# Fewer TensorE transposes and low-word pieces, per-head exponentials and a new order in a fused attention and SoLU kernel

## The chip, the cores and the metric

The kernel runs on one core of a Trainium2 chip. The metric is device time in microseconds (us). PE is TensorE, DVE VectorE, ACT ScalarE, POOL GpSimd, SP SyncE, whose queue here issues the loads and the DMA transposes. SBUF is the on-chip memory, and PSUM the accumulators that TensorE writes.

## The reference

Chunked attention over 4 batches, 8 heads, 768 positions, head size 64, followed by a SoLU layer. Every chunk of 32 queries sees 8 memory keys and a window of 16 + 32 + 8 keys (64 in all).

```python
for c in range(nc):                                   # 24 chunks of 32 queries
    scores = scale * q_c @ k_full.T                   # k_full: memory + window
    a = np.exp(scores - max(scores))
    out[c] = (a / (sum(a) + 1e-9)) @ v_full
x = out as (3072 tokens, 512)
h = x @ w_in                                          # 512 -> 1024
solu = h * softmax(h)
ln = (solu - mean) / sqrt(var + 1e-6) * g_ln
return ln @ w_out                                     # 1024 -> 512
```

All tensors are float32. The kernel uses a faster matmul type of 32 bits that keeps fewer mantissa bits, so that each operand of the two dense products is split in a high and a low part, and three products are summed.

## The kernel before

The 3072 tokens make 24 tiles of 128. Attention works on 13 units: tiles 0 and 1 alone, then pairs of tiles. The whole program is one list of steps, written out by hand in a string called `ORDER` and executed in that order under a manual schedule: every engine gets its instructions in the order in which the steps name them, and semaphores hold back an instruction whose data or buffer is not ready. The number in a step is its unit, tile or weight piece; the letter after @ is its engine (V DVE, S ACT, G POOL, Y SP).

Weights come in 16 pieces of 128 x 512 elements (0 to 7 of `w_in`, 8 to 15 of `w_out`), each element as 8 bytes, the two 32-bit words of a double. Steps on a piece `i`:

- `D` loads the raw words (512 KB). `A` (ACT, `w_pack`) and `B` (DVE, `w_first`) make the leading value from the high word, `E` (DVE, `w_exp`) its power of two.
- `H` (`w_high`) writes the rounded high part, for `w_out` scaled by `g_ln`.
- `T` (DVE, `w_word`) makes the contribution of the low word in one instruction with two factors.
- `R` (`w_rest`) adds value, minus high part and low word in PSUM by three matmuls of 512 columns with identity or diagonal matrices; `W` (ACT) copies the sum to the low part. There are two such PSUM buffers.
- For the other pieces `K`, `Y` and `J` do the same by element-wise steps on POOL or DVE without PE.

Attention steps of a unit: `S` scores, `M` row maxima, `Bm` scores minus maximum, `X` exponentials in place, `Z` their sums and inverses. Then the probabilities are transposed, either on PE (`PT`, with `PC` copying the result from PSUM) or by a DMA transpose (`Ps` splits the words in two planes of 16 bits, `Px` is the DMA, `Pm` joins the planes). `V` multiplies by the values, `N` normalises, and the result is transposed in the same two ways (`XT`, or `Xs`, `Xx`, `Xm`) and split in high and low parts (`XH`, `XL`).

Dense steps of a tile: `G` is the first product in four parts by `w_in` (12 matmuls of 128 x 512 for two halves, a quarter of the depth each: 6 per part); `Hm`, `He`, `Hu`, `Sq`, `C` are maximum, exponential, product with sums, squares, and centring; `UT`, or `Us`, `Ux`, `Um`, transposes; `UH`, `UL` split; `O` is the second product in eight parts of three matmuls; `Os` and `St` scale and store.

Buffers of one kind are handed out first in, first out in program order: 12 SBUF `slot` tiles, 8 rounded tiles `fr`, 3 PSUM tiles `two`, 2 PSUM tiles `one`, and two each for q, k and v. A step that takes a buffer waits until its previous user has finished.

Of the kernel before, what the change touches and what calls it, by code (L numbers as in the profile page):

```python
# [35 lines left out]
W3@S M2 G1.0 D8 G0.0 W2@S B4 E5 H5@S G1.1 Bm2 A6 E4 T5 H4@S A7 Lk4@Y B6 T4 X2 G0.1 R4 R5 D9 Z2 S3
H6@S D10 B7 E6 A9 E7 T7 W4@S T6 R6 W5@S M3 H7@S G1.2 A8 Lv2@Y B8 Bm3 G0.2 E8 R7 B9 Lq4@Y PT2 D11
W6@S X3 E9 W7@S T8 A10 T9 PC2 H9@S Z3 G0.3 Hm0 H8@S D12 V2 B10 A11 G1.3 Lq5@Y D13 N2 E10 He0 A12 XT2
Hm1 A13 B11 R8 K10@G H10@S R9 Hu0 Y10@G E11 XH2@S Sq0 B12 He1 XL2@V PT3 K11@V Dn0@G PC3 Lk6@Y S4
Lv3@Y E12 C0 Hu1 B13 G2.0 M4 G2.1 Lv4@Y K12@G H11@S T10 H12@S Sq1 Y12@G E13 K13@G G2.2 Bm4 V3 G2.3  # L40
Lk5@Y J10@G T12 C1 X4 H13@S W8@S N3 G3.0 W9@S XT3 G3.1 G3.2 Hm2 Ps4.0@S Z4 Lv5@Y Y11@G XH3@S XL3@V
Y13@G J12@G Ps4.1@G D14 Dn1@G Lq7@Y G3.3 He2 Hu2 Px4 UT0 D15 T11 Sq2 Hm3 UH0@S J11@G He3 C2 UL0@V
G4.0 Dn2@G Pm4.0@G G4.1 Us2.0@S A14 T13 O0.0 A15 Hu3 Us2.1@G S5 O0.1 Sq3 Pm4.1@S B14 G4.2 E14 B15
Ux2 O0.2 J13@G Dn3@G E15 G4.3 K14@V H14@S UT1 O0.3 K15@G T14 M5 O0.4 Bm5 H15@S UH1@S Y14@G Y15@G
O0.5 J14@V UL1@V Um2.0@G V4 N4 Um2.1@G X5 Ps5.0@S UH2@G Ps5.1@S Xs4.0@S Xs4.1@S T15 O0.6 G5.0 O1.0
J15@V G5.1 Lq6@Y O1.1 Hm4 C3 Us3.0@S G5.2 Px5 He4 Z5 O1.2 Xx4 O1.3 Us3.1@G O0.7 G5.3 Pm5.0@G UL2@V
Os0 Hu4 Sq4 O1.4 Hm5 Ux3 S6 Lk7@Y O2.0 Xm4.0@G O1.5 O2.1 Lk8@Y C4 He5 Lv6@Y Pm5.1@G O1.6 St0 Xm4.1@S
Dn4@G O2.2 O2.3 O2.4 M6 Us4.0@G O1.7 Um3.0@S Bm6 XH4@G O2.5 V5 X6 Um3.1@G Os1 Ps6.0@S Us4.1@G UH3@S
Ux4 XL4@V Hu5 N5 O2.6 Sq5 UL3@V G6.0 O2.7 Z6 G6.1 S7 G7.0 C5 Ps6.1@G Xs5.0@S Px6 Xs5.1@S Dn5@G G6.2
Xx5 O3.0 G6.3 Us5.0@S Us5.1@G Os2 Um4.0@S G7.1 O3.1 St1 Pm6.0@S Hm6 Um4.1@G He6 G7.2 UH4@S Xm5.0@S  # L50
Pm6.1@G O3.2 Hu6 G7.3 Xm5.1@G Sq6 O3.3 UL4@V O3.4 Ux5 Um5.0@G V6 Hm7 O4.0 C6 Lq8@Y O3.5 XH5@S O3.6
Um5.1@S XL5@V Dn6@G O4.1 N6 Us6.0@S He7 Hu7 St2 UH5@S O3.7 UL5@V Xs6.0@G G8.0 Sq7 Us6.1@G O4.2 G8.1
# [622 lines left out]
```

## Time and profile before

| | |
|---|---|
| median of 3 runs | 352.19 us (351.4 to 353.33) |
| profiled execution | 352.38 us, span 350.6 us, mean clock 0.983 |
| PE | 338.9 us busy (97%), 4368 matmuls |
| DVE, ACT, POOL | 230.2, 203.4, 201.5 us busy |
| DMA | 62.90 MB, mean 179 GB/s |
| first product of the dense layer starts | 27.14 us |
| PE is idle between 27 us and the last matmul | 2.1 us in all |

The profiled execution lies 0.2 us above the median, and its time 1.8 us above its span, the part before the first and after the last instruction. A matmul on PE overlaps its neighbours, so the distance from one start to the next is read as its cost, and the listed duration is longer.

### The profile page before, as it was taken

The page shows a single profiled execution, that of the slowest core. Times are in us where ns is not written, and L with a number is a line of the kernel's source. Part 1 is how long each engine was busy: PE and PEld are TensorE (multiplying, and loading weights), DVE is VectorE, ACT ScalarE, POOL GpSimd, SP SyncE. Part 2 cuts the span into 40 slices and gives each one's busy share as a digit, 9 for nine tenths or more (in the row PEclk, how much of TensorE's full clock was granted, in tenths as well). Part 3 has the DMA queues.
Part 4 walks back from the last instruction along what each step waited for, and adds up shares of the span by engine and source line. Part 5 has one row for each costly group of instructions (what it writes and reads, how often), then busy time and mean ns, then how long its engine had stood idle before and what let it go on. Part 6 is the DMA issues. An engine that isn't in the chain of part 4 may idle for free.

```text
span 350.6 us, 9994 instructions
## 1 busy us (share of the span) xinstructions
PE 338.9 (97%) x4368; PEld 269.4 (77%) x4368; DVE 230.2 (66%) x298; ACT 203.4 (58%) x265; POOL 201.5 (57%) x231
## 2 busy tenths in 40 slices
PE   7599999999999999999999999999999999999995
...
PEclk9679999999999999999999999999999999999999
...
GB/s 230 409 310 407 284 345 118 283 125 113 201 254 190 143 84 194 339 158 166 218 209 197 263 192 153 227 130 169 245 89 68 60 91 107 76 127 53 2 90 60
DMA packets 96907, 62.90 MB, mean 179 GB/s; under 512 B 82528, under 2 KB 82528, under 8 KB 96864
## 3 DMA queue, kind: packets, MB, share of 16 engines
...
## 4 chain that ended last, share of the span: by engine, by line
PE 88%; DVE 7%; DMA 2%; ACT 1%; issue 1%; SPq 0%
PE one L570 39%; PE two L509 35%; PE two L400 9%; PE one L309 2%; DMA slot<-in_w_in 2%; PE two L380 2%; DVE per_row L518 1%; DVE slot L533 1%; DVE slot L470 1%; DVE slot L551 1%; DVE fr L301 1%; DVE fr L229 1%; PE one L310 1%; PE one L311 1%; SPq L236 0%
## 5 line engine op out<-in xcount | busy, mean ns | idle before, releaser
L223 POOL TENSOR_SCALAR slot<-slot 128x1024 uint16<-128x1024 uint16 x94 | 119.5, 1297 | 53.6 <-DVE slot L551 16.2
L570 PE MATMUL one<-w_out_h,fr 128*128 128x512 f32 x384 | 133.8, 399 | 0.0
L509 PE MATMUL two<-w_in_h,fr 128*128 128x512 f32 x384 | 133.4, 398 | 0.3 <-ACT two L541 0.3
L509 PEld LDWEIGHTS two<-w_in_h,fr 128*128 128x128 f32 x384 | 72.2, 188 | 17.8 <-ACT two L541 0.5
L570 PEld LDWEIGHTS one<-w_out_h,fr 128*128 128x128 f32 x384 | 72.2, 188 | 17.6
L221 ACT COPY slot<-slot 128x1024 uint16<-128x1024 uint16 x62 | 71.7, 1195 | 15.7 <-DVE slot L551 10.0
L509 PE MATMUL two<-w_in_l,fr 128*128 128x512 f32 x192 | 75.7, 394 | 0.0
L570 PE MATMUL one<-w_out_l,fr 128*128 128x512 f32 x192 | 75.7, 394 | 0.0
L518 DVE TENSOR_REDUCE per_row<-two 128x1 f32<-128x1024 f32 x24 | 29.3, 1222 | 41.0 <-PE two L509 41.0
L229 DVE TENSOR_TENSOR fr<-slot,fr 128x1024 fp32r<-128x1024 f32 x30 | 45.6, 1526 | 6.0 <-PE one L570 2.1
L523 ACT ACTIVATE slot<-two,per_row 128x1024 f32<-128x1024 f32 x24 | 26.8, 1116 | 38.8 <-DVE per_row L518 36.5
L509 PEld LDWEIGHTS two<-w_in_l,fr 128*128 128x128 f32 x192 | 36.2, 188 | 8.1
L570 PEld LDWEIGHTS one<-w_out_l,fr 128*128 128x128 f32 x192 | 36.1, 188 | 8.0
L578 ACT ACTIVATE o_sb<-one,per_row 128x512 f32<-128x512 f32 x24 | 16.4, 685 | 34.5 <-PE one L570 34.5
L541 ACT ACTIVATE two<-slot,per_row 128x1024 f32<-128x1024 f32 x24 | 26.8, 1118 | 13.9 <-DVE per_row L536 13.8
L533 DVE CUSTOM_DVE_ANT_0 slot<-two,slot 128x1024 f32<-128x1024 f32 x24 | 29.2, 1215 | 8.1 <-ACT slot L523 8.0
L551 DVE TENSOR_SCALAR slot<-slot,per_row 128x1024 f32<-128x1024 f32 x24 | 23.2, 965 | 11.1 <-ACT two L541 11.1
L470 DVE TENSOR_TENSOR slot<-two,per_head 128x1024 f32<-128x1024 f32 (+1 forms) x13 | 14.8, 1140 | 11.3 <-PE two L400 11.3
L400 PEld LDWEIGHTS two<-v,slot 64*32 64x32 f32 x1536 | 16.6, 108 | 5.6 <-issue 4.8
L319 POOL TENSOR_SCALAR slot<-slot,g_col 128x512 f32<-128x512 f32 x4 | 3.3, 821 | 29.7 <-DVE slot L284 28.1
L400 PE MATMUL two<-v,slot 64*32 64x64 f32 x1536 | 19.0, 232 | 0.7 <-issue 0.7
L400 PEld LDWEIGHTS two<-k,q 64*32 64x32 f32 x1536 | 16.4, 105 | 4.3 <-issue 3.3
...
## 6 DMA issues: line engine op xcount, KB each, us to landing
...
k<-in_kw SPq DMA_DIRECT2D x11, 672.0 KB, 5.2
out<-o_sb ACTq DMA_DIRECT2D x24, 256.0 KB, 2.4
q<-in_qT SPq DMA_DIRECT2D x11, 512.0 KB, 4.8
slot<-in_w_in SPq DMA_DIRECT2D x8, 512.0 KB, 9.1
slot<-in_w_out SPq DMA_DIRECT2D x8, 512.0 KB, 5.6
v<-in_vw SPq DMA_DIRECT2D x2, 512.0 KB, 10.8
k<-in_kw SPq DMA_DIRECT2D x2, 336.0 KB, 4.6
```

Source lines behind the costliest of these rows:

```text
L221: nc.scalar.copy(out, in_)
L223: nc.gpsimd.tensor_scalar(out, in_, 1.0, 0.0, ALU.mult, ALU.add)
L229: either(on).tensor_tensor(out, a, b, ALU.subtract)
L400: nc.tensor.matmul(out[32 * j:32 * j + 32, r, t, g], *pairs(slice(r * D, (r + 1) * D), t, g, j), start=True, stop=True,)
L470: nc.vector.tensor_tensor(x, heads(u, get("xp", u), D).rearrange("p r t g n -> p r (t g) n"), rinv.broadcast_to([P, 2, n, D]), ALU.mult,)
L509: nc.tensor.matmul(h[:, half], x[a], w[b][:, c, half * HALF:(half + 1) * HALF], start=c == 0 and i == 0, stop=c == NC_ - 1 and i == 2,)
L518: nc.vector.tensor_reduce(take("per_row", ("hm", t), 1), flat(get("h", t)), axis=AX.X, op=ALU.max, negate=True)
L523: nc.scalar.activation(take("slot", ("u", t), 3), flat(get("h", t)), AF.Exp, bias=get("hm", t), scale=1.0, accum_out=take("per_row", ("esu ...
L533: nc.vector.tensor_tensor_reduce(u, flat(get("h", t)), u, 1.0, 0.0, ALU.mult, ALU.add, accum_out=usum)
L541: nc.scalar.activation(flat(get("h", t)), get("u", t), AF.Square, bias=get("nmu", t), scale=1.0, accum_out=take("per_row", ("var", t), 1),)
L551: nc.vector.tensor_scalar(u, u, get("nmu", t), None, ALU.add)
L570: nc.tensor.matmul(get("o", t), u[a], w[b][:, f], start=f == 0 and i == 0, stop=f == NF - 1 and i == 2)
```

## The change

- `PT2`, `PT3` (probabilities of units 2 and 3) and `UT0`, `UT1` (tiles 0 and 1 of the dense layer) become DMA transposes: `Ps`, `Px`, `Pm` and `Us`, `Ux`, `Um`. `UT23`, `PT0`, `PT1` and the four `XT` stay.
- Pieces 8 and 9 lose `R` and `W` and go the way of `K`, `Y`, `J`; the diagonal matrices `Dg` go.
- Units 0 and 1 use `Mh` (maxima, times the scale), `Xh` (an exponential instruction for each of 8 heads, 64 wide, straight from PSUM with a bias and a sum) and `Zh` (inverses) for `M`, `Bm`, `X`, `Z`.
- The low word of five pieces (3 to 7) goes to POOL in two instructions, `Tc` (word to float, scaled, in place) and `Tp` (times the power of two). Nine of the `H` go from ACT to POOL (before none).
- `C` may run on POOL (4 of 24 do), with two operations in the instruction for one. 14 `slot` tiles for 12.
- `ORDER` is another list throughout.

```diff
-SLOTS, ROUNDED = 12, 8
+SLOTS, ROUNDED = 14, 8
-SCALED = range(10, 16)
+SCALED = range(8, 16)
 ORDER = """
-CT Lq0@Y Lq1@Y Lk0@Y Lk1@Y Wu16 D0 D1 A0 Lv0@Y S0 D3 Lv1@Y D2 S1 M0 Lg Bm0 D4 M1 X0 A1 Bm1 Z0 Lq2@Y
+Lk0@Y CT Lk1@Y Lq0@Y Wu16 S0 Mh0 D3 A3 Xh0 B3 Lq1@Y D7 PT0 A7 PC0 D1 E3 S1 Lv0@Y V0 A1 B7 E7 Zh0 Mh1
...
+    def w_word_f32(i, on):
+        f = piece(i)[3]
+        factor = g_word[:, f:f + 1] if i in SCALED else 2.0**-52
+        low = word(i, 0)
+        if on == "S":
+            nc.scalar.activation(low.bitcast(F32), low, AF.Copy, scale=factor)
+        else:
+            either(on).tensor_scalar(low.bitcast(F32), low, factor, 1.0, ALU.mult, ALU.mult)
+
+    def w_word_exp(i, on):
+        p = get("a", i)[:, HALF:]
+        t = take("fr", ("t", i), 1)[:, 0:HALF]
+        either(on).tensor_tensor(t, word(i, 0).bitcast(F32), p, ALU.mult)
+        used("raw", i)
...
+    def exps_by_head(u):
+        s = heads(u, get("s", u), KEYS)
+        nmax = per_head(u, get("nmax", u))
+        sums = per_head(u, take("per_head", ("rinv", u), 1))
+        n = len(UNITS[u]) * NP_
+        a = take("slot", ("p", u), 2)[:, 0:2 * n * KEYS]
+        for i in range(n):
+            for r in range(2):
+                k = 2 * i + r
+                nc.scalar.activation(
+                    a[:, k * KEYS:(k + 1) * KEYS], s[:, r, i // NP_, i % NP_], AF.Exp,
+                    bias=nmax[:, r * n + i:r * n + i + 1], scale=scale, accum_out=sums[:, k:k + 1],
+                )
...
+    def scaled_max(u):
+        row_max(u)
+        nmax = per_head(u, get("nmax", u))
+        nc.vector.tensor_scalar(nmax, nmax, scale, None, ALU.mult)
+
+    def inverses(u):
+        s = per_head(u, get("rinv", u))
+        nc.vector.tensor_scalar(s, s, 1e-9, None, ALU.add)
+        nc.vector.reciprocal(s, s)
...
-    def u_center(t):
+    def u_center(t, on):
         u = get("u", t)
-        nc.vector.tensor_scalar(u, u, get("nmu", t), None, ALU.add)
+        if on == "S":
+            nc.scalar.activation(u, u, AF.Identity, bias=get("nmu", t), scale=1.0)
+        else:
+            either(on).tensor_scalar(u, u, get("nmu", t), 0.0, ALU.add, ALU.add)
```

The order on PE, from the warm-up on, before. `two` and `one` are the PSUM tiles, k, q, v the inputs; L400 are scores (from k, q) and values (from v), L380 transposes, L309 to L311 the three matmuls of an `R`, the end of the list is `S2`.

```order
L400 MATMUL two_81<-k_88,q_86 32x64 x32
L400 MATMUL two_82<-k_89,q_87 32x64 x32
L380 MATMUL two_83<-ident,slot_66 128x128 x4
L380 MATMUL two_81<-ident,slot_69 128x128 x4
L400 MATMUL two_82<-v_90,slot_70 32x64 x32
L380 MATMUL two_83<-ident,slot_70 128x128 x4
L400 MATMUL two_81<-v_91,slot_66 32x64 x32
L309 MATMUL one_84<-slot_63,ident 128x512
...
L400 MATMUL two_81<-k_88,q_86 32x64 x64
```

The same place now (L418 for L400, L398 for L380, L327 for L309):

```order
L418 MATMUL two_83<-k_90,q_88 32x64 x32
L398 MATMUL two_84<-ident,slot_63 128x128 x4
L418 MATMUL two_85<-k_91,q_89 32x64 x32
L418 MATMUL two_83<-v_92,slot_66 32x64 x32
L327 MATMUL one_86<-slot_62,ident 128x512
L328 MATMUL one_86<-w_in_h,eye_neg 128x512
L329 MATMUL one_86<-fr_76,eye 128x512
L418 MATMUL two_84<-k_90,q_88 32x64 x64
L398 MATMUL two_83<-ident,slot_71 128x128 x4
L327 MATMUL one_87<-slot_65,ident 128x512
```

The scores of unit 1 now come after the transpose of unit 0, and the scores of unit 2 after one `R` for three; in all seven `R`, for four, and also `S3`, stand ahead of the first `G`.

On POOL, after the constants, before (the first rows make `g_word` and the diagonal matrices, then comes `K10`):

```order
L200 TENSOR_SCALAR g_word<-g_col 128x8
L204 TENSOR_SCALAR diag<-ident,g_col 128x128
L205 TENSOR_SCALAR diag_r<-ident,g_col 128x128
...
L319 TENSOR_SCALAR slot_62<-slot_62,g_col 128x512
L324 TENSOR_TENSOR slot_62<-slot_62,w_out_h 128x512
```

And now (L314 is `Tc`, L319 `Tp`, L225 to `w_in_h` is `H`):

```order
L314 TENSOR_SCALAR slot_61<-slot_61 128x512
L225 TENSOR_SCALAR w_in_h<-slot_62 128x512
L319 TENSOR_TENSOR fr_76<-slot_61,slot_62 128x512
...
L319 TENSOR_TENSOR fr_82<-slot_63,slot_67 128x512
L225 TENSOR_SCALAR w_in_h<-slot_74 128x512
L319 TENSOR_TENSOR fr_77<-slot_66,slot_64 128x512
L225 TENSOR_SCALAR slot_70<-slot_71 128x1024
L202 TENSOR_SCALAR g_word<-g_col 128x8
```

Sixteen instructions on weight pieces of `w_in`, and one of the two planes for `Px2`, now stand ahead of what was first on POOL.

On SP, the issues of loads and transposes from the 24th on, before:

```order
L236 DMA v_90<-in_vw 128x2x1024
L236 DMA q_86<-in_qT 128x2x512
L268 DMA slot_61<-in_w_out 128x1024
L268 DMA slot_66<-in_w_out 128x1024
L236 DMA q_87<-in_qT 128x2x512
```

And now:

```order
L270 DMA slot_62<-in_w_out 128x1024
L238 DMA q_88<-in_qT 128x2x512
L270 DMA slot_71<-in_w_out 128x1024
L379 DMA_TRANSPOSE slot_61<-slot_70 128x16x128
L238 DMA v_92<-in_vw 128x2x1024
L270 DMA slot_64<-in_w_out 128x1024
L379 DMA_TRANSPOSE slot_73<-slot_74 128x16x128
```

Two transposes (`Px2`, `Px3`) stand among the loads of `w_out` and v; before, the first transpose was the 37th issue.

More of the change, by code (lines that the diff above doesn't have):

```diff
@@ L36 @@
[L36 to L52, printed above, removed]
@@ L88 @@
-Os19 O21.0 O21.1 O20.5 UH23@S Dn23@G UL23@V O21.2 O20.6 O21.3 O20.7 Os20 O21.4 O21.5 O22.0 O21.6
-O22.1 Dn22@G O21.7 O22.2 O22.3 St20 Os21 O23.0 O22.4 O23.1 O22.5 O23.2 St21 O23.3 O23.4 O22.6 O23.5
-St19 O22.7 Os22 O23.6 St22 O23.7 Os23 St23
+Lk0@Y CT Lk1@Y Lq0@Y Wu16 S0 Mh0 D3 A3 Xh0 B3 Lq1@Y D7 PT0 A7 PC0 D1 E3 S1 Lv0@Y V0 A1 B7 E7 Zh0 Mh1
+D0 B1 Tc3@G E1 T1 H3@G A0 B0 N0 Tp3@G H7@G Lq2@Y Xh1 Tc7@G D2 A2 Lk2@Y Zh1 B2 E0 Tp7@G R3 S2 E2 D4
+XT0 D6 A4 R7 W3@S H1@S D5 A6 A5 T0 H0@G Lq3@Y W7@S T2 R0 Lk3@Y M2 XH0@S Bm2 B5 PT1 B6 B4 Tc6@G W0@S
@@ new lines @@
+Tc4@G R1 S3 Lv1@Y E5 Lg PC1 Tc5@G H5@G H4@G X2 Tp5@G D10 D9 Ps2.0@S E4 D11 E6 H6@S Tp4@G H2@G V1 R5
+W1@S XL0@V R4 W5@S Lk4@Y Z2 A10 N1 Tp6@G Ps2.1@G M3 B10 A9 XT1 XH1@S Bm3 D15 B9 A11 X3 W4@S R2 Dw
+E10 Lq4@Y B11 E9 E11 G0.0 R6 K9@G H9@G K11@G A15 W2@S D13 W6@S S4 XL1@V G0.1 G0.2 G0.3 T10 T9 B15
+Px2 Lv2@Y Ps3.0@S T11 M4 E15 Ps3.1@S Z3 D8 A13 Px3 Pm2.0@S Bm4 K10@G Y9@G Pm2.1@S G1.0 H10@S K15@G
+J9@G A8 X4 H11@G Lv3@Y Hm0 He0 V2 Lv4@Y T15 G1.1 B13 N2 Y10@G XT2 XH2@S Z4 D12 Hu0 XL2@V Sq0 Pm3.0@G
@@ new lines @@
+Y11@G Pm3.1@G G1.2 G1.3 V3 Hm1 Ps4.0@G B8 He1 A12 Lk6@Y E13 C0@G N3 Lq5@Y Hu1 G2.0 G2.1 J10@G E8
+Ps4.1@S XT3 Lk5@Y Px4 Sq1 K13@G G2.2 XH3@S Us0.0@G Us0.1@S T13 C1@G Us1.0@S G2.3 K8@G S5 B12 T8 E12
+Pm4.0@S XL3@V Hm2 J11@G G3.0 G3.1 M5 He2 Bm5 G3.2 G3.3 Us1.1@G Ux0 H15@G Pm4.1@S Lk7@Y Ux1 Y15@G
+H8@S V4 Hu2 Lq6@Y Sq2 G4.0 K12@V H13@S G4.1 Um0.0@G Hm3 N4 G5.0 He3 Um0.1@G T12 Y13@G Xs4.0@G X5
+UH0@S Y8@V Lv7@Y H12@S Hu3 Xs4.1@S J8@V Um1.0@G Um1.1@G Ps5.0@S Dn1@G D14 UL0@V Y12@V G5.1 Sq3
+Ps5.1@S Lq7@Y C2@V Us2.0@G UH1@S G4.2 O0.0 G4.3 O0.1 J12@V Xx4 A14 C3@G Us2.1@G G5.2 J13@V S6 Hm4
```

89 lines of the change are left out of this document (50 added, 39 removed).

## The prediction

> **What bounds the kernel now.** I read first the page's shares, slices and clock, then the chain that ended last, then PE's waits.
>
> ```profile
> PE 338.9 (97%) x4368; PEld 269.4 (77%) x4368; DVE 230.2 (66%) x298; ACT 203.4 (58%) x265; POOL 201.5 (57%) x231
> PE   7599999999999999999999999999999999999995
> PEclk9679999999999999999999999999999999999999
> PE 88%; DVE 7%; DMA 2%; ACT 1%; issue 1%; SPq 0%
> ```
>
> PE is full from the third slice on and the chain runs through it. From about 18 us the end moves with the amount of work in PE's list and with PE's few waits; what DVE, ACT and POOL do counts only where PE waits for them. Those waits, from 45 to 110 us (later slices are full):
>
> ```profile
> PE two L400 <- issue: 0.7, 1, 0.7
> PE two L380 <- ACT two L541: 0.7, 1, 0.7
> PE two L380 <- DVE slot L470: 0.4, 1, 0.4
> PE two L509 <- ACT two L541: 0.3, 1, 0.3
> ```
>
> 2.1 us is all that better ordering behind the head can win. What is left is work taken off PE, and the head, where PE waits for loads.
>
> **Work taken off PE.** From the chain (start, length), `PT2` and `UT1`; from the timeline, the stretch with `R8`, `R9`, `PT3` and then `S4`, and `UT0` and the `G` behind it:
>
> ```profile
> 42.71 0.87 PE two L380 x8
> ...
> 79.92 0.87 PE two L380 x8
> ```
>
> ```profile
> 48.72 1.02 PE L309 MATMUL one<-slot,diag 128*128 128x512 f32 x2
> 52.26 1.09 PE L380 MATMUL two<-ident,slot 128*128 128x128 f32 x8 [0.72 <-ACT two L541]
> 53.28 1.48 PE L400 MATMUL two<-k,q 64*32 64x64 f32 x128
> 69.04 1.03 PE L380 MATMUL two<-ident,slot 128*128 128x128 f32 x8
> 70.34 0.50 PE L509 MATMUL two<-w_in_h,fr 128*128 128x512 f32 x1 [0.27 <-ACT two L541]
> ```
>
> `PT2` and `UT1` are 0.87 each. From 48.72 to 53.28 all is removed: 4.56, of it two `R` at about 1.3 each, a transpose, and 0.72 of waiting for the transpose's PSUM buffer. `UT0` takes 70.34 - 0.27 - 69.04 = 1.03. Together 0.87 + 0.87 + 4.56 + 1.03 = 7.3 us. The 0.27 in front of `G4.0` is a wait for a buffer that the dense layer itself holds; I keep it.
>
> **The head.** In-order loads set it. Sizes, and when loads of the kernel before had landed (ACT waiting for the third and fifth weight piece, then issue and landing of the k of units 2 and 3):
>
> ```profile
> k<-in_kw SPq DMA_DIRECT2D x11, 672.0 KB, 5.2
> ...
> q<-in_qT SPq DMA_DIRECT2D x11, 512.0 KB, 4.8
> slot<-in_w_in SPq DMA_DIRECT2D x8, 512.0 KB, 9.1
> ...
> v<-in_vw SPq DMA_DIRECT2D x2, 512.0 KB, 10.8
> k<-in_kw SPq DMA_DIRECT2D x2, 336.0 KB, 4.6
> ...
> q<-in_qT SPq DMA_DIRECT2D x2, 256.0 KB, 2.8
> ```
>
> ```profile
> 14.89 0.66 ACT L274 ACTIVATE slot<-slot 128x512 f32<-128x512 f32 x1 [1.41 <-DMA slot<-in_w_in]
> ...
> 18.88 0.68 ACT L274 ACTIVATE slot<-slot 128x512 f32<-128x512 f32 x1 [0.20 <-DMA slot<-in_w_in]
> ```
>
> ```profile
> L236 SPq DMA_DIRECT2D k<-in_kw x1: 379/379/379, 13.6 to 13.6; - x1
> ...
> DMA to landing us min/median/max: 9.4/9.4/9.4
> ```
>
> ```profile
> L236 SPq DMA_DIRECT2D k<-in_kw x1: 433/433/433, 21.7 to 21.7; - x1
> ...
> DMA to landing us min/median/max: 7.5/7.5/7.5
> ```
>
> Added up in issue order, these are 3232 KB at 14.9, 4768 at 18.9, 6464 at 13.6 + 9.4 = 23.0 and 8672 at 21.7 + 7.5 = 29.2: a straight line of some 390 KB per us. In the new list v of unit 0 ends at 3232 KB (14.9), k of unit 2 at 5440 KB (20.5), k of unit 3 at 8160 KB (27 to 28) and v of unit 1 at 8672 KB (28.3 to 29.2; the old line lost about 1 us to an issue that waited for an SBUF slot, and there are two more slots now).
>
> PE's own rows of the head: the first `R` at a low clock (twice the 1.02 of 48.72), scores of unit 2, the first `G`.
>
> ```profile
> 18.21 2.07 PE L309 MATMUL one<-slot,ident 128*128 128x512 f32 x2
> ...
> 24.30 1.48 PE L400 MATMUL two<-k,q 64*32 64x64 f32 x128
> ...
> 27.14 0.39 PE L509 MATMUL two<-w_in_h,fr 128*128 128x512 f32 x1
> ```
>
> The per-head exponentials, priced from full-width rows: plain 512 and 1024 wide, with bias 1024 wide, and the read of the sum.
>
> ```profile
> L440 ACT ACTIVATE slot<-slot 128x1024 f32<-128x1024 f32 x11 | 11.7, 1059 | 11.1 <-DVE slot L431 11.1
> ...
> L440 ACT ACTIVATE slot<-slot 128x512 f32<-128x512 f32 x2 | 1.2, 622 | 0.0
> ```
>
> ```profile
> L523 ACT ACTIVATE slot<-two,per_row 128x1024 f32<-128x1024 f32 x24 | 26.8, 1116 | 38.8 <-DVE per_row L518 36.5
> ...
> L523 ACT ACTIVATION_READ_ACCUMULATOR slot<-two,per_row 128x1 f32 x24 | 4.6, 192 | 0.0
> ```
>
> 437 ns for 512 columns leave about 185 ns fixed; with 57 for the bias and 55 for 64 columns one is 0.30 us, plus 0.19 for the read, at most 8 x 0.49 = 3.9 us a unit; neighbours on ACT overlap by about 0.1, twice here, so at least 8 x 0.26 = 2.1. I take 2.3, since it is many short ones in a row. The old path of a unit (`Bm`, `X`) is one instruction on DVE and 0.62 on ACT, so `PT0` comes 1 to 2 us later. It does not matter: the first piece (1440 KB, not after 10.3 on this line), 0.66, 2.3 and a cold transpose of 1.1 give 14.4 at the latest, with the scores of unit 1 (about 1.2 cold) 15.6, and V0 waits for v until 14.9 anyway. V0 ends near 16.1 to 16.8, R3 at half clock near 19. Then the list has `S2`, whose k lands at 20.5, and `XT0`, `R7`, `R0` behind it must wait with it: over 1 us of idle PE.
>
> From there at full clock: S2 1.4, XT0 0.45, R7 and R0 2.6, PT1 0.45, R1 1.3: 26.7. S3 waits for k until 27 to 28, 1.4 more; V1 ends at 29.2 to 29.9; R5, R4, XT1, R2 take 4.4: the first `G` at 33.6 to 34.3. If the low clock lasts until 24.5, it is up to 35.5. Equal work in the old kernel would be at 27.14 plus three `R` (4.0) plus S3 (1.6) = 32.7. The head costs 0.9 to 2.8 us; I take 2.0. By the Trainium skill, page "TensorE: Matmul & The Clock Gate", section "What's actually happening", an idle window of about 3.4 us halves the clock and a busy one restores it; the trace's 0.6 and 0.7 in slices 2 and 3 and the doubled `R` agree, and by that rule the wait for `S2` would keep the clock low, the upper of the two ends (348.8 for the sum).
>
> **Low words and high parts on POOL, `K` `Y` `J` for two pieces.** Rows for a scaling and for a two-input operation on POOL, and a short DVE shift alone and beside POOL, DVE's full-width reduction, and DVE's busy time from 45 to 75 us:
>
> ```profile
> L319 POOL TENSOR_SCALAR slot<-slot,g_col 128x512 f32<-128x512 f32 x4 | 3.3, 821 | 29.7 <-DVE slot L284 28.1
> ...
> L324 POOL TENSOR_TENSOR slot<-slot,w_out_h 128x512 f32<-128x512 f32 x6 | 8.7, 1464 | 1.7 <-ACT w_out_h L221 0.8 <-DVE per_row L536 0.8
> ```
>
> ```profile
> 46.17 0.42 DVE L279 TENSOR_SCALAR slot<-slot 128x512 uint32<-128x512 uint32 x1
> ...
> 74.62 1.26 DVE L279 TENSOR_SCALAR slot<-slot 128x512 uint32<-128x512 uint32 x1
> ```
>
> ```profile
> L518 DVE TENSOR_REDUCE per_row<-two 128x1 f32<-128x1024 f32 x24 | 29.3, 1222 | 41.0 <-PE two L509 41.0
> ```
>
> ```profile
> 45.00:75.00 30.00, 29.65 (x44) 1.00 0.74 238
> ```
>
> `Tc` (an integer input, no row) lies between 0.82 and 1.46; nearest is 0.82, a scaling with the same shape. Five `Tc`, five `Tp`, six `H` are 5 x 0.82 + 5 x 1.46 + 6 x 0.82 = 16.3 us on an engine that was idle there (28.1 us before its first row). After piece 5 (6976 KB, 24.5) Tc5, H5, H4, Tp5, Tp4 end at 29.9, H2 and Tp6 at 32.2, just ahead of R4 (30.5), R2 and R6: hidden, with about 1 us to spare. At twice these durations `R4` would be 4 us late. Moving 5 of 16 low words (one instruction each) frees some 3 us of DVE, and fewer `H` free ACT.
>
> Of pieces 8 and 9, K, Y, J (0.8 to 1.5 us each) lie beside some 30 us of `G`, before the first `O`, and cost nothing; nor do the four `C` on POOL, or the second operation in `C`.
>
> **DMA transposes for PE's.** Each adds two splits and two joins (about 1.1 us each on ACT or POOL), and a transfer. `Px2` is issued behind a `w_out` piece that takes the slot of Ps2's source, about 35; with a queue of 3 us ahead and 3 of its own it lands near 41, the v behind it near 44, the joins on ACT end at 43.5. PE, from the first `G` at 34.6 with R6, S4, G0.1 to G1.0, comes to `V2` near 45.5. That is 2 us of cover.
>
> **DVE in the dense start.** It was busy for 29.65 of 30 us (the row above). In the new list DVE has, from `Hm0` to `UL0`, 17 full-width instructions at 1.22 less some 0.08 of overlap, 13 half-width ones (six at 0.42, seven estimated at half of a full one, 0.6), and small ones for 2 us: 28 us; PE has 17 `G` parts (1.4), four attention steps (1.6) and two transposes to do before `O0.0`: 32 us. A few hits by POOL (0.84 in the row of 74.62) take 3 us, so 1 us of cover stays. For these two thin covers and R6's wait for a copy I add 0.9 us.
>
> Sum: 352.4 (this execution; the median is 0.2 below) - 7.3 + 2.0 + 0.9 = 348.0.
>
> **Rivals.** *The head costs nothing* (loads without the old gap come 2 us earlier, the clock is back at 18): 352.4 - 7.3 = 345.1, and 344.4 with the 0.7 of the other buffer waits. For it speaks the gap, against it that `V1` needs 8672 KB.
>
> *Transposes late in the load rush.* Weight pieces took 9.1 us at the median to land and v loads 10.8. Px2 issued at 35 would land at 44 to 46, V2 begin at 48 to 49 and PE idle 3 us, and `Px3` with `V3` a second time for 1: 348 + 4 = 352, no change. Against it: four loads at most are ahead of it.
>
> *POOL slows DVE* (slower). The shift above took 1.26 for 0.42. If DVE's 28 us stretch by a factor f, `UL0` is late by 28f - 32, and `O0.0` with it; at f = 1.39 it is 6.9 us, which takes all of 347.1 to 354.0; at 1.5 it is 10 us and 357. Against it: the mean of DVE's long reduction is 1.22 over all 24 tiles, with POOL busy for 57% of the span. The Trainium skill, page "SBUF — State Buffer", section "Who interferes with whom", states that GpSimd and a VectorE operation in a two-port mode, or with two SBUF inputs, exclude each other for a whole instruction; the row at 74.62 agrees, the full-width ones read PSUM.
>
> **Numbers.** Forecast 0.60, free head 0.14, late transposes 0.15, POOL against DVE 0.11. Half a percent (1.8 us) is what a measurement here tells from no change: faster is below 350.4, 0.74; same 0.15; slower 0.11. The range reaches from the free head, 344.4, to the late transposes, 352.5.
>
> **What would show it.** Right: first `G` at 33.5 to 35.5, PE waiting for k ahead of `S2`; `PT2`'s place filled; PE busy without a gap over 1 us from 46 us on; 40 transposes on PE for 72. Wrong: PE waiting for POOL's `fr` at R4 or R6, for the join at `V2`, or for `UL0` at `O0.0`; the last matmul later than 345.

## The result, and the profile after

The change makes the kernel slower: 361.62 us median (359.88 to 362.55) against 351.99 us for the kernel before on the same chip, a ratio of 1.0256 with a 95% interval of 1.0227 to 1.0285. The prediction was 348.0 us. The profiled execution took 362.43 us, span 360.6.

The page: busy time of the engines, PE and the granted clock in 40 slices (9 us each), the instruction queue among the DMA queues, and the chain that ended last.

```profile
PE 336.6 (93%) x4328; PEld 265.8 (74%) x4328; DVE 232.3 (64%) x291; ACT 217.9 (60%) x299; POOL 232.2 (64%) x251
...
PE   7359968989989999999999999999999999999995
...
PEclk9666999999999999999999999999999999999999
...
q8 instruction: 34, 0.56, 0.6%
...
PE 73%; POOL 7%; DMA 6%; DVE 6%; issue 4%; ACT 2%; SPq 0%; POOLq 0%; ACTq 0%; DVEq 0%
```

PE's busy time fell by 2.3 us only (338.9 to 336.6), although the list is shorter: slices 2 to 4 stand at a clock of 0.6, where the kernel before had two lower ones (0.6 and 0.7). And PE is idle for 24.0 us of the span (360.6 - 336.6) in place of 11.7. Its waits, all of the run:

```profile
PE two L418 <- issue: 8.4, 4, 3.7
PE two L398 <- ACT slot L470: 3.2, 4, 2.4
PE two L554 <- issue: 2.7, 1, 2.7
PE two L554 <- DVE fr L231: 2.2, 2, 1.2
```

"issue" means that PE waited for nothing that the profile shows. It was 0.7 us before and is 11.1 us now. The timeline shows where: V0 is cut after 57 of its 64 products, S2 after 117 of 128, the second `G` part (`G0.1`) after 4 of 6 matmuls, V2 after 107 of 128. The row at 41.69 is the first `G`.

```profile
13.84 1.11 PE L418 MATMUL two<-v,slot 64*32 64x64 f32 x57
18.52 0.43 PE L418 MATMUL two<-v,slot 64*32 64x64 f32 x7 [3.57 <-issue]
...
21.74 1.66 PE L418 MATMUL two<-k,q 64*32 64x64 f32 x117
27.11 0.45 PE L418 MATMUL two<-k,q 64*32 64x64 f32 x11 [3.71 <-issue]
...
41.69 0.40 PE L554 MATMUL two<-w_in_h,fr 128*128 128x512 f32 x1
...
48.04 0.63 PE L554 MATMUL two<-w_in_h,fr 128*128 128x512 f32 x2
51.34 0.50 PE L554 MATMUL two<-w_in_l,fr 128*128 128x512 f32 x1 [2.67 <-issue]
...
56.19 1.30 PE L418 MATMUL two<-v,slot 64*32 64x64 f32 x107
58.39 0.42 PE L418 MATMUL two<-v,slot 64*32 64x64 f32 x21 [0.91 <-issue]
```

V0, S2 and V2 find each of their inputs in one tile, so that a cut in their middle is no wait for data. Counted in the trace (a matmul and its weight load are two instructions), the cuts stand right behind PE's 449th, 705th, 1473rd and 1729th instruction, all of the form 193 + 256 n. Together these four take 3.57 + 3.71 + 2.67 + 0.91 = 10.9 us; a fifth issue wait of 0.27 us, ahead of V3, stands at no such place. The page's queue q8 moves 0.56 MB in 34 transfers, 16 KB each, and PE has 8718 instructions, some 34 times 256. (The Trainium skill, page "Runtime: NRT & Kernel Launch", section "What's in a NEFF", gives TensorE's stream as raw instructions of 64 bytes; 256 of them are 16 KB, so the trace agrees.) Worked out from the records of q8 and of PE, in us:

```
kernel   border  PE enters the    block that starts   PE reaches   PE goes
                 block before it  at it has landed    the border   on at
before     449        6.95              12.2              14.8       14.8
before     705       14.8               19.3              24.6       24.6
before     961       24.6               28.8              33.8       33.8
after      449        7.9               17.1              14.6       18.5
after      705       18.5               25.8              23.2       27.1
after     1473       46.0               50.1              48.3       51.3
after     1729       51.3               57.1              57.3       58.4
```

The request for a block is in no record. These rows fit one that is made when PE enters the block before it: the new block lands 4 to 9 us after that, while data loads run, and a PE that stands there goes on some 1.3 us behind the landing. In the first 60 us of all the runs below the time from entering to landing was 1.5 to 9.2 us. Later in the span some blocks land before PE enters the block before, up to 3.9 us earlier, so there the request comes ahead of PE's work. In these rows, then, 256 instructions must last as long as the next block takes. Sixty-four or 128 small products of `S` or `V` are 128 or 256 instructions in 0.8 to 1.5 us; a `G` part is 12 in 1.4 us. From border 449 to border 705 PE takes 9.8 us in the list before (14.8 to 24.6) and 4.7 in the new one (18.5 to 23.2). The cut at 449 is of another kind: PE spends 6.7 us on the block ahead of it (7.9 before), but the next block lands at 17.1 us for 12.2.

Two more things are new. SP's queue, start and length, with the two DMA transposes of units 2 and 3 and v of unit 2 between them; and `C` on GpSimd beside a 128 x 1024 scaling on VectorE (mean ns behind the busy time):

```profile
40.56 6.18 SPq L379 DMA_TRANSPOSE slot<-slot  x1
46.80 0.57 SPq L238 DMA_DIRECT2D v<-in_vw  x1
...
47.98 6.64 SPq L379 DMA_TRANSPOSE slot<-slot  x1
```

```profile
L599 POOL TENSOR_SCALAR slot<-slot,per_row 128x1024 f32<-128x1024 f32 x4 | 16.2, 4051 | 0.7 <-ACT two L586 0.7
```

A transpose held SP's queue for over 6 us (3.17 for the first one of the kernel before), and `C` takes 4.05 us on GpSimd (0.97 on VectorE before, with one operation; 1.05 on VectorE now, with two).

The chain that ended last holds both kinds of loss. Its own pieces (start, length):

```profile
14.95 3.57 issue
...
23.40 3.71 issue
...
40.56 17.58 DMA slot<-slot x2
...
64.49 3.72 POOL slot L599
```

The first two cuts are on it. From 40.56 to 58.14 us it runs through the two DMA transposes instead, past the cuts in `G0.1` and V2; the joins of `Px3` on GpSimd begin at 58.94, right behind V2's end at 58.8, so that the transposes and the cuts came to nearly the same time there. Then it goes through three of the four `C` on GpSimd (two more at 71.77 and 104.17).

### The profile page after: what moved, and what is told of

Same layout as the page of the kernel before. It is cut to its first block, busy times and chain, and to the rows that moved or that the text cites. A ratio compares the mean times of both kernels' runs of the same rounds, so it can differ in the third digit from the quotient of the medians.

```text
span 360.6 us, 10003 instructions
## 1 busy us (share of the span) xinstructions
PE 336.6 (93%) x4328; PEld 265.8 (74%) x4328; DVE 232.3 (64%) x291; ACT 217.9 (60%) x299; POOL 232.2 (64%) x251
## 4 chain that ended last, share of the span: by engine, by line
PE 73%; POOL 7%; DMA 6%; DVE 6%; issue 4%; ACT 2%; SPq 0%; POOLq 0%; ACTq 0%; DVEq 0%
PE one L618 35%; PE two L554 27%; PE two L418 7%; DMA slot<-slot 5%; POOL slot L599 3%; POOL slot L225 2%; PE one L327 2%; DMA q<-in_qT 2%; DVE fr L231 1%; DVE slot L578 1%; PE two L398 1%; POOL w_out_l L346 1%; ACT slot L470 1%; DVE w_out_l L346 1%; DVE per_head L440 1%
## 5 line engine op out<-in xcount | busy, mean ns | idle before, releaser
L225 POOL TENSOR_SCALAR slot<-slot 128x1024 uint16<-128x1024 uint16 x87 | 114.1, 1334 | 58.1 <-DMA slot<-slot 25.7
L618 PE MATMUL one<-w_out_h,fr 128*128 128x512 f32 x384 | 131.6, 397 | 0.7 <-DVE fr L231 0.7
L223 ACT COPY slot<-slot 128x1024 uint16<-128x1024 uint16 x85 | 98.4, 1199 | 25.9 <-DMA slot<-slot 10.8
L231 DVE TENSOR_TENSOR fr<-slot,fr 128x1024 fp32r<-128x1024 f32 x32 | 49.6, 1556 | 23.0 <-POOL fr L225 12.9
L563 DVE TENSOR_REDUCE per_row<-two 128x1 f32<-128x1024 f32 x24 | 29.2, 1217 | 26.2 <-PE two L554 26.2
L626 ACT ACTIVATE o_sb<-one,per_row 128x512 f32<-128x512 f32 x24 | 16.4, 685 | 46.6 <-PE one L618 43.7
L554 PEld LDWEIGHTS two<-w_in_l,fr 128*128 128x128 f32 x192 | 36.2, 188 | 10.9 <-issue 3.1
L586 ACT ACTIVATE two<-slot,per_row 128x1024 f32<-128x1024 f32 x24 | 26.8, 1118 | 14.4 <-DVE per_row L581 14.3
L225 POOL TENSOR_SCALAR fr<-slot 128x1024 fp32r<-128x1024 f32 x21 | 24.4, 1161 | 16.4 <-ACT slot L223 12.5
L599 DVE TENSOR_SCALAR slot<-slot,per_row 128x1024 f32<-128x1024 f32 x20 | 20.8, 1050 | 15.4 <-ACT two L586 15.4
L418 PEld LDWEIGHTS two<-k,q 64*32 64x32 f32 x1536 | 17.0, 109 | 9.8 <-issue 7.3
L418 PE MATMUL two<-k,q 64*32 64x64 f32 x1536 | 19.5, 233 | 4.8 <-issue 3.7
L418 PE MATMUL two<-v,slot 64*32 64x64 f32 x1536 | 18.9, 229 | 4.8 <-issue 4.7
L418 PEld LDWEIGHTS two<-v,slot 64*32 64x32 f32 x1536 | 16.4, 107 | 9.5 <-issue 7.7
```

What stands on the lines that cost most here:

```text
L223: nc.scalar.copy(out, in_)
L225: nc.gpsimd.tensor_scalar(out, in_, 1.0, 0.0, ALU.mult, ALU.add)
L231: either(on).tensor_tensor(out, a, b, ALU.subtract)
L418: nc.tensor.matmul(out[32 * j:32 * j + 32, r, t, g], *pairs(slice(r * D, (r + 1) * D), t, g, j), start=True, stop=True,)
L554: nc.tensor.matmul(h[:, half], x[a], w[b][:, c, half * HALF:(half + 1) * HALF], start=c == 0 and i == 0, stop=c == NC_ - 1 and i == 2,)
L563: nc.vector.tensor_reduce(take("per_row", ("hm", t), 1), flat(get("h", t)), axis=AX.X, op=ALU.max, negate=True)
```

## Experiments

Ratios are against the kernel before on the same chip, with 95% intervals. Theory A: PE waits for its own instructions, at block borders.

**Fewer warm-up instructions.** `Wu16` becomes `Wu8`, or goes. Nothing else changes but the place of the borders in the program. (A token is two matmuls with their weight loads, so that eight tokens are 16 matmuls and 32 PE instructions; the two texts below call the instructions matmuls.)

```diff
-Lk0@Y CT Lk1@Y Lq0@Y Wu16 S0 Mh0
+Lk0@Y CT Lk1@Y Lq0@Y Wu8 S0 Mh0
```

> The changed kernel with 8 instead of 16 warm-up tokens: 32 dummy matmuls fewer ahead of S0, no other instruction changed. Theory A (PE's instructions come in blocks of 256 through a DMA queue, behind the data loads): the borders of the blocks move 32 instructions later in the program, from the 57th product of V0 to before R3 (instruction 449 becomes 481), from inside S2 to R7, from G0.1 to G0.2. The waits named issue then lie elsewhere; the one in V0 comes 32 instructions later and is partly covered, and G0.1's goes or shrinks. Time about 355 to 359. Rival B (the waits come from data or from the list's order, not from the blocks): the same waits at the same tokens, S0 colder, 361 to 363.

Measured 358.22 us, 1.0149 (1.0129 to 1.0169), 3.4 us below the changed kernel. PE's timeline:

```profile
23.08 0.74 PE L325 MATMUL one<-slot,ident 128*128 128x512 f32 x1
26.44 0.91 PE L325 MATMUL one<-slot,ident 128*128 128x512 f32 x1 [2.62 <-issue]
...
38.94 0.40 PE L552 MATMUL two<-w_in_h,fr 128*128 128x512 f32 x1
...
49.76 1.43 PE L416 MATMUL two<-v,slot 64*32 64x64 f32 x123 [0.42 <-ACT w_out_h L221]
54.01 0.39 PE L416 MATMUL two<-v,slot 64*32 64x64 f32 x5 [2.82 <-issue]
```

V0 and S2 are whole, `R7` is cut between its first two matmuls and V2 after 123 products: instructions 705 and 1729 again, 32 later in the program. That is what theory A says and rival B excludes. Of the time won in V0, part went to waits for loads (2.9 for q ahead of S0, 2.5 for k ahead of S2).

> The changed kernel without the 64 dummy matmuls ahead of S0. Theory A: borders 64 instructions later: in place of 449, 705, 961, 1473 they stand at 513, 769, 1025, 1537. No issue wait inside V0 or inside S2 at 117 products; one may come in the first third of S2 and one ahead of S3. Time 354 to 359, and issue waits of another size and at other tokens. Rival B: the same waits at the same tokens; a colder clock in S0 to V0 adds 1 us: 362 to 364.

Measured 362.54 us, 1.0266 (1.021 to 1.0322). The cuts left V0 and S2, as theory A said, and now stand between S3 and V1 (961), in XT2 (1729) and in V3 (1985), 10.2 us in three waits: a shift moves them, it doesn't remove them. The time is the one that rival B gave, since I had counted the borders that vanish and not those that fall on V1, XT2 and V3; the wait for q ahead of S0 also grew, to 5.9 us.

**Undoing parts of the change.** The four `C` on VectorE (`C0@G` becomes `C0@V`, and so on):

> The changed kernel with the four C (C0, C1, C3, C4: 3.7 us each on GpSimd in the changed kernel) on VectorE again. Theory A (fetch waits and late transposes in the first 60 us made the loss): POOL is 15 us less busy from 60 to 110 us, PE's waits from 75 to 107 us shrink by 1 to 2 us, time 359.5 to 361.5. Rival C (GpSimd became the bound of the dense start): 4 us or more come back, 355 to 358. Rival D (VectorE is the bound there): it has 4 us more to do and PE waits longer, 363 to 365.

1.0157 (1.0107 to 1.0208); four executions lie between 357.3 and 365.4 us, too scattered to tell A from C; repeated below on a steadier base. The transposes of units 2 and 3 on PE again:

```diff
-G0.2 G0.3 ... Px2 Lv2@Y Ps3.0@S ... Pm2.0@S ... XL2@V Sq0 Pm3.0@G
+G0.2 PT2 G0.3 ... Lv2@Y ... A13 PC2 ... XL2@V PT3 Sq0 PC3
```

> The changed kernel with the transposes of units 2 and 3 on TensorE again, and without their splits, joins and DMA transposes. Theory A: PE's block borders from instruction 1465 on move by 8 to 16, the wait in G0.1 stays, v of unit 2 is issued 6 us earlier, V2 no longer depends on a join; 1.74 us of work back on PE, 2 to 3 us of waiting ahead of V2 gone; 359 to 362. Rival E (the two DMA transposes in the load rush, which hold SP's queue for 6 us each, are the main cause): 352 to 356. Rival F (the transposes are hidden): 363.4, the 1.74 us of work and nothing else.

365.3 us, 1.038 (1.0314 to 1.0447): slower than all three theories said. No join stands ahead of V2 any more, but 449, 705, 1473 and, with 1.6 us, 2753 still cut the list, and PT3 now waits for a PSUM tile.

```profile
PE two L415 <- issue: 6.4, 2, 3.2
PE two L551 <- issue: 3.8, 2, 2.2
PE two L395 <- DVE fr L228: 2.9, 1, 2.9
```

So the DMA transposes are not the main cause: without them the issue waits still sum to 10.2 us. Nor does this run price them, since the cut at 2753 and PT3's wait are new in it.

**More slots alone.** The kernel before with `SLOTS = 14`:

> The kernel before with 14 slot tiles for 12, nothing else. Weight loads are issued earlier, more of them stand in the DMA queues. Theory A (instruction blocks stand behind the data loads in flight): the first blocks of PE's instructions come 1 to 3 us later than before (11.2, 18.2, 27.9 us), but PE's small products lie further apart there, so at most 2 us of issue waits: 351.5 to 354. Rival (the deeper prefetch by itself is the fault of the change): 355 or more, with issue waits of several us in V0 to S2.

0.9995 (0.9966 to 1.0024), the first block lands at 12.6 us for 12.2. The prefetch by itself is not at fault.

**Parts of the change alone, in the kernel before.** Pieces 8 and 9:

```diff
+SCALED = range(8, 16)
-... E8 ... E9 ... R8 K10@G H10@S R9 ... W8@S W9@S     (Dg0, Dg1 gone too)
+... E8 K8@G ... E9 K9@G ... Y9@G J9@G Y8@G J8@G K10@G H10@S
```

> The kernel before with one part of the change alone: pieces 8 and 9 go the way of K, Y, J on GpSimd, and R8, R9, W8, W9 and two diagonal matrices are gone. PE's list is 2.6 us shorter, and PT3 finds its buffer 0 to 0.7 us later or earlier. The prediction's term says 2.6 to 3.4 us faster: 349.0 to 350.0. Rival (nothing to win, since K, Y, J make O0.0 or H late): 351.5 to 353.

354.44 us, 1.0049 (1.0026 to 1.0072): slower, although PE's list is 2.6 us shorter. One wait, ahead of `PT3`, grew from 0.7 to 5.2 us:

```profile
PE two L378 <- ACT two L539: 5.2, 1, 5.2
```

Its PSUM tile is freed by `Sq0` on ScalarE. In ScalarE's queue `H10` stands ahead of `Sq0` and waits for `K10` on GpSimd, which now stands behind `Y8` and `J8` (`K10` on GpSimd, then `H10`, `XH2` and `Sq0` on ScalarE):

```profile
50.48 0.69 POOL L317 TENSOR_SCALAR slot<-slot,g_col 128x512 f32<-128x512 f32 x1
```

```profile
51.20 0.62 ACT L219 CAST w_out_h<-slot 128x512 fp32r<-128x512 f32 x1 [2.21 <-POOL slot L317]
51.73 1.01 ACT L219 CAST fr<-two 128x1024 fp32r<-128x1024 f32 x1
52.63 1.12 ACT L539 ACTIVATE two<-slot,per_row 128x1024 f32<-128x1024 f32 x1
```

Placed better, with `K`, `H`, `Y` and `J` of both pieces on GpSimd and right behind `E8`, `E9` and `T9`:

> Pieces 8 and 9 by element on GpSimd once more, now H too on GpSimd and all steps ahead of K10, so that no H on ScalarE waits behind K. By the prediction's term 2.6 to 3.4 us faster: 349 to 350.5. Rival (the two R filled a time in which PE would have waited for Sq0 anyway: PT3 needs a PSUM tile that Sq0 frees at 52.1 us, and Sq0 hangs on VectorE's Hu0): PT3 starts at 51.5 to 52.3 as before, 352 to 353.

353.92 us, 1.0043 (1.002 to 1.0066), PT3 at 54.5 us: the rival by its time, and a little worse, as PT3 was to start by 52.3. `K10` still came 2.6 us later than before, behind the new steps on GpSimd. That the two `R` had filled a time in which PE had nothing else to do is not shown by this run, since PT3 came late for a reason of its own.

`UT0` and `UT1` as DMA transposes (`Us0` behind `C0`, `Ux0` behind `Lk5`, `Um0` ahead of `UH0`; the same for tile 1), alone, and together with pieces 8 and 9:

> The kernel before with one part of the change alone: UT0 and UT1 as DMA transposes (and 14 slots, which alone changed nothing). PE's list is 1.9 us shorter. By the prediction's term 350.0 to 351.5. Rival (from 45 to 80 us VectorE is busy all the time, PE waits for UH, UL or an SBUF slot instead, and Lv5 and D14 queue behind Ux0 on SP): 352.5 to 355.

> The head of the kernel before (order, M, Bm, X, Z, T on VectorE, PT2 and PT3 on PE, all C on VectorE) with those parts of the change that lie behind the load rush: pieces 8 and 9 element-wise, UT0 and UT1 as DMA transposes, 14 slots. PE's work is 2.6 + 0.87 + 1.03 us shorter. Theory A: no new issue wait in the head, 346.5 to 348.5, faster than both kernels. Rival (splits and joins stretch VectorE or come late for O0.0): 349 to 353.

354.83 us, 1.0075 (1.0046 to 1.0105), and 359.45 us, 1.0193 (1.0133 to 1.0253). Together, `PT3` waits 5.2 us once more, and two new cuts take 1.6 us at border 2497 and 0.8 at 3777, besides waits of the `O`. Alone, PE's list is 1.9 us shorter, and the `O` wait 3.6 us for `UH0`, a low part of `w_out` and `UL0`:

```profile
PE one L568 <- ACT fr L219: 1.9, 1, 1.9
PE one L568 <- DVE w_out_l L326: 1.2, 1, 1.2
...
PE one L568 <- DVE fr L227: 0.5, 1, 0.5
```

**Small products further apart.** The changed kernel with `Wu8`, S2 behind `R0`, S3 behind `R4`, S4 behind `G0.1`:

```diff
-R3 S2 E2 D4 XT0 D6 A4 R7 ... R0 Lk3@Y M2 ... R1 S3 Lv1@Y ... S4 XL1@V G0.1 G0.2
+R3 E2 D4 XT0 D6 A4 R7 ... R0 S2 Lk3@Y M2 ... R1 Lv1@Y ... R4 ... S3 M3 ... XL1@V G0.1 S4 G0.2
```

> The changed kernel with 8 warm-up tokens and with S2 behind R0, S3 behind R4 and S4 behind G0.1, each of them further from its neighbours with small products. The same instructions. Theory A: 256 small instructions no longer fall into less time than a block needs to come; the issue waits of the first 45 us, 11.1 us in the changed kernel, fall below 4, first G at 35 to 38 (41.7 in the changed kernel, 38.9 with 8 warm-up tokens alone); V2 still waits for its DMA transpose; 354 to 357. Rival B (data set the waits): first G at 39 or later, 358 or more.

360.2 us, 1.0216 (1.0154 to 1.0279). Half right: no cut in the head, first `G` at 37.5 us. But V2 is cut at border 1729 with 5 products to go, and ends at 55.1, later than with `Wu8` alone (54.4). The 1.4 us won in the head were lost there. The 1.0 ahead of V2 is at no border: VectorE's `Bm4` frees V2's PSUM tile at 49.9.

```profile
37.53 0.40 PE L552 MATMUL two<-w_in_h,fr 128*128 128x512 f32 x1
...
50.01 1.42 PE L416 MATMUL two<-v,slot 64*32 64x64 f32 x123 [1.02 <-issue]
54.80 0.31 PE L416 MATMUL two<-v,slot 64*32 64x64 f32 x5 [3.37 <-issue]
```

Then `Wu8` once more, ahead of `R6`, to have V2's block asked for earlier; and besides that `Bm4` ahead of `Z3`:

> The list of the run before with spread small products, and 8 dummy tokens (32 useless PE instructions, some 1.3 us of work) added ahead of R6, where PE waits 1.1 us for the copy of a low part. They move the block border 1473 from G0.2 to the end of S4 and the border 1729 from the last 5 products of V2 to its 107th, so that the block that V2 needs is asked for some 3 us earlier. Theory A: V2's issue wait of 3.4 us falls to 0 to 0.5, V2 ends at 51.5 to 52 for 55.1, time 356.5 to 357.5, though PE does more. Rival B (no effect of the borders): 360.5.

> The same, and on VectorE Bm4 ahead of Z3, so that the PSUM tile that V2 takes is free at 47.6 instead of 49.9 us. If V2's start then hangs on nothing but PE, V2 starts at 49 and ends at 50.5, 1 us less than the run without it: 355.5 to 356.5. Rival (the DMA transpose of unit 2 and its joins come just as late): no difference.

360.54 us, 1.0234 (1.02 to 1.0267), and 360.53 us, 1.0229 (1.0199 to 1.0259). My times were wrong, and so was the remedy. Border 1473 came to lie 2 products before the end of S4 and cost 2.0 us there (PE had entered the block before only 2.1 us earlier, as S4's 256 instructions fill it), and the next block took 7.8 us from PE's entering to its landing, so that V2 was cut after all (1.8 and 0.4 us). The theory of the borders holds in both; how long a block takes I can't forecast: from 1.5 to 9.2 us in the first 60 us of all the runs.

What these lists have in common is the rest of the program. From the end of V2 to the end of the span it takes 301.8 us in the changed kernel, and 302.2, 302.5, 302.7 and 302.6 with `Wu8`, spread, and with the dummies. Whatever is won ahead of V2 counts only as far as V2 ends earlier.

**Which engine for `C`.** The kernel with `Wu8`, C0, C1, C3 and C4 on VectorE, or on ScalarE:

> The changed kernel with 8 warm-up tokens and C0, C1, C3, C4 on VectorE. In the run with 8 warm-up tokens PE waited 3.0 us for UL and XL of VectorE between 70 and 103 us, behind C of 3.7 us on GpSimd. Theory C (C on GpSimd makes the transposed tile late): 1 to 3 us faster than 358.2: 355 to 357. Rival D (VectorE is itself the bound): 358 to 360.

> The same with those four C on ScalarE (1.1 us each by the squares' rows, in place of 3.7 us on GpSimd or 0.8 on VectorE). If the engine of C matters at all, the best of the three: 355 to 356.5. If not: 358.

360.28 us, 1.0206 (1.0168 to 1.0243), and 357.08 us, 1.0113 (1.008 to 1.0147), against 1.0149 with `C` on GpSimd. Theory C falls: VectorE is no better place. That fits rival D (one wait of 2.7 us for its `XL` in place of two of 0.6 and 1.0); that VectorE is the bound there is argued, not shown. ScalarE is the best of the three by about 1 us, at the edge of what the intervals tell apart; the stretch behind V2 is 301.0 us in that run.

```profile
L595 ACT ACTIVATE slot<-slot,per_row 128x1024 f32<-128x1024 f32 x4 | 4.6, 1145 | 0.0
```

**The clock of the head, in the kernel before.** Dummies in PE's waits; then C0 to C2 on ScalarE too; then fewer warm-up tokens, so that border 961 comes later:

```diff
-Wu16 ... S1 M0 ... PT0 B0 ... V0 Z1 ... C0 ... C1 ... C2
+Wu16 ... S1 Wu7 M0 ... PT0 Wu3 B0 ... V0 Wu2 Z1 ... C0 ... C1 ... C2              (first run)
+Wu16 ... S1 Wu7 M0 ... PT0 Wu3 B0 ... V0 Wu2 Z1 ... C0@S ... C1@S ... C2@S        (second run)
+Wu10 ... S1 Wu7 M0 ... PT0 Wu3 B0 ... V0 Wu2 Z1 ... C0@S ... C1@S ... C2@S        (third; Wu8: fourth)
```

> The kernel before with 12 dummy tokens (48 useless PE instructions) in the three waits of its head: 7 behind S1, 3 behind PT0, 2 behind V0. They move the block borders 28 to 48 instructions forward, where no stall stands near (the blocks land 2.6 to 7 us ahead of need in the head of the kernel before). If the low granted clock of 0.55 from 10 to 20 us is only the price of those waits, R3's neighbours V0 to R1 run at full clock: V0, V1, two transposes and two R take 5 us for 7.7, of which loads and copies give some back: 350.5 to 352, 1 to 2 us faster than before. Rival: S2's k lands at 23.0 us in any case and the rest of the head waits for it: 352.5 to 353.5.

> The same, and C0, C1, C2 on ScalarE (one activation with a bias each) for VectorE, which is busy 99% of 50 to 80 us while ScalarE is busy for 68%. If VectorE's load makes PE's waits of 1.3 us there, 0.5 to 1 us faster than the run without it: 349.5 to 351.5. Rival: C stands behind Sq on ScalarE and makes U late: no difference, or 1 us slower.

353.27 us, 1.0009 (0.9988 to 1.003), and 351.36 us, 0.9973 (0.9946 to 1.0). The granted clock from 10 to 20 us rose from 0.55 to 1.00 (last but two in a row of the view by windows; before, then second run), yet the first run won nothing: it had a new wait.

```profile
10.00:20.00 10.00, 7.12 (x143) 4.72 (x143) 7.77 (x20) 6.47 (x12) 2.23 (x5) 0.55 1.01 397
```

```profile
10.00:20.00 10.00, 8.33 (x167) 6.19 (x167) 9.53 (x22) 8.01 (x14) 2.90 (x5) 1.00 1.03 404
```

```profile
31.36 0.73 PE L507 MATMUL two<-w_in_h,fr 128*128 128x512 f32 x2 [3.06 <-issue]
```

It stands at instruction 961: PE, 48 instructions further on through the dummies, reached it at 27.9 us, and the block landed at 29.8. PE also waited 2.3 us for k, as the rival said. In the second run the border was reached at 25.9, its block landed at 26.9, and it cost 2.0 us, so that 1.1 us of the second run's gain over the first may be this wait and not `C`. The last two runs only move that border back:

> The kernel before with dummies in the waits of the head and C0 to C2 on ScalarE, as in the run before, but 10 warm-up tokens for 16: 24 PE instructions fewer ahead of S0. In that run PE stood 2.0 us (3.1 in the one without C) at the block border 961, which the 48 added dummies had pulled from 33.8 us, where the kernel before reaches it, to 25.9 us, ahead of its block (landed at 26.9). With 24 fewer it is reached at about 28.7, some 0.4 us behind the resumption seen there. Theory A: no issue wait over 0.5 us in the head, 1.5 to 2 us faster than the run before: 349.4 to 350.2, faster than both kernels by over 0.5%. Rival B (the borders don't matter; the colder start costs): 351.5 to 352.5.

> The same with 8 warm-up tokens: border 961 another 8 instructions later, at about 29.6 us, 1.3 us behind the resumption. Theory A: the same time as with 10 tokens, 349.2 to 350.4, and more evenly, since the border has a margin. Rival B: 352 or more, since S0 and S1 run colder.

349.77 us, 0.9919 (0.9891 to 0.9947), and 349.82 us, 0.9906 (0.9876 to 0.9936): as theory A said, with 24 or 32 instructions fewer and 2.0 us less of waiting at 961, which PE passes at 28.5 us with its block there since 27.0 (run with `Wu10`). One cut of 0.9 us is left at border 1217, more than the 0.5 that theory A allowed. These two runs bundle dummies, `C` on ScalarE and the shorter warm-up; `C` on ScalarE was not tried here alone. Both beat the kernel before by 0.8 to 0.9% and the changed one by 3%. What issue waits remain are short (the page's clock row, and PE's waits, of the run with `Wu10`):

```profile
PEclk9999999999999999999999999999999999999999
```

```profile
PE two L398 <- DMA k<-in_kw: 2.6, 2, 1.6
PE two L398 <- issue: 1.5, 3, 0.9
```

## Why the prediction was wrong

Against the profiled execution the miss is 362.4 - 348.0 = 14.4 us. V2 is the place to split it. By the prediction's numbers V2 begins at 45.5 and ends at 47.0, with 346.2 - 47.0 = 299.2 us of span behind it. It ended at 58.8, with 301.8 behind it. So 11.8 us were lost up to V2 and 2.6 behind it.

- **The step that failed first** is the reading of PE's waits: "2.1 us is all that better ordering behind the head can win", and `issue: 0.7` passed over as part of it. That row is PE waiting for a block of instructions (it stands at instruction 3521, also of the form 193 + 256 n). In the kernel before, each of the next blocks had landed before PE came to its border (12.2 for 14.8, 19.3 for 24.6, 28.8 for 33.8 us); the new order was priced as if instructions were always there. Measured in its place: 10.9 us of waits at borders of instruction blocks, 3.57 + 3.71 in the head, 2.67 at `G0.1`, 0.91 in V2. That these waits are for instructions is shown by the run with `Wu8`: 32 instructions fewer ahead of them, the cuts at 705 and 1729 stand 32 instructions later in the program, those in V0 and `G0.1` are gone, and the time is 3.4 us shorter. Why the blocks came when they did is not shown.
- **The head: +2.0, first `G` at 34.6** (33.6 to 35.5). Measured 41.69, 7.1 us late, where the two cuts of V0 and S2 are 7.28. The wait for k ahead of `S2` that I forecast did not show: the cut in V0 brought PE to S2 only at 21.7 us, when its k was there. With V0 whole (`Wu8`) it did, 2.5 us. With the cuts gone (spread list) the first `G` came at 37.5, so that some 3 us of the head were missing in my working even so. The waits there are 3.0 us for tiles that VectorE normalises, 1.8 for copies of low parts, 1.4 for GpSimd's low words, which I had called hidden, and 0.7 for `Bm`; the 2.0 had no term for them. One term is also added up wrongly: 0.49 less 0.2 is 0.29, so that the lower bound of eight exponentials is 2.3 us and not 2.1; the sum used 2.3.
- **The cover of V2: +0.9.** From the first `G` to V2 I counted 10.9 us; 14.5 were measured, of which 2.67 are a cut and 0.85 a wait of S4; the rest, 11.0, is what I had counted. The rival "transposes late in the load rush" had the condition right (Px2 issued at 40.6 for 35, SP held 6.2 us, landed 10.6 us after its issue where I assumed 6), but V2 did not wait for the joins: they ended at 53.8 and V2 began at 56.2, late through the cuts. The chain does run through the transposes from 40.56 on, so they stood close behind the cuts; what they cost by themselves is open, since no run of the new list has the cuts away and these transposes on PE.
- **Work taken off PE: -7.3.** The work did go (40 transposes for 72, no `R8`, `R9`); the time followed in part. Behind V2 the span was 304.2 us before. The new list has two parts of `G` more there (2.8) and one `S` less (1.4): 305.6, and 6.5 of the 7.3 us should have come off. It took 301.8, so 3.8 came off and 2.6 were lost to waits. Tried alone in the list before, the terms for `R8`, `R9` and for `UT0`, `UT1` have the wrong sign: +1.4 and +2.6 us against their reference, for -2.6 and -1.9; there other work stands in the queues, so this does not measure the terms in the changed kernel. I took PE's 97% for the bound. From 45 to 75 us PE and VectorE were both full, three PSUM tiles link them, and in the runs alone the work taken from PE became a wait: 5.2 us for `Sq0`, 3.6 us ahead of the `O`. The sentence on `K`, `Y`, `J`, "cost nothing", left out who is queued behind them.
- **`C` on GpSimd: "nothing".** 4.05 us each, a size that the prediction did not look up. Three of them are on the chain. But moving them to VectorE gave nothing and to ScalarE some 1 us: the effect was small. (The Trainium skill, page "GPSIMD Engine Reference", section "4.1 Engine selection", calls one-input operations there roughly line-rate; this one, with a column as operand, took 4.05 us for 1.05 on VectorE with the same two operations, and the measurement decides.)
- **The clock.** The sentence that a wait ahead of `S2` would keep it low was right in kind, but the two cuts did it and not that wait: two idle windows of 3.6 and 3.7 us, clock 0.6 up to 36 us. It made the work off PE nearly invisible in the busy time.
- **Terms that held:** the exponentials by head took 2.3 us a unit, eight of them from 9.77 to 12.1 us; `Tc` 0.65 and `Tp` 1.37 (0.82 and 1.46 assumed); PE never waited for them in the changed kernel. They were not tried alone.
- Rival "POOL slows DVE" did not decide it: PE's waits for VectorE behind V2 sum to 3.2 us, and VectorE's long reduction kept its mean (1.22 before, 1.21 now).

What stays open: why a block needs 1.5 us in one place and 9 in another. The first block landed at 16.4 to 17.5 us in all runs on the changed list, whether PE had entered the block before at 7.9 or at 13.2 us, and at 12 to 14 in those on the old list. It is not simply behind the loads that were issued earlier: in the kernel before it landed at 12.2 us, ahead of a weight piece that was issued at 4.0, before PE entered the block, and landed at 14.9. The order of the loads differs between the two lists, and no run changed it alone or took loads away.
